# Row sums of W_tok: on VectorE from the rows as loaded, or on TensorE from the transposed matrix

## The chip, the core and the metric

The kernel runs on one core of a Trainium2 chip. A core has a matrix engine (TensorE, in the profile PE, with its weight loads as PEld), three engines for elementwise work (VectorE: DVE; ScalarE: ACT; GpSimd: POOL), a sync engine that issues transfers (SP), and 16 DMA engines. Each engine works through its own instructions in a fixed order and waits on semaphores for the others. Matmuls write to PSUM, eight banks of 2 KB per partition; everything else lives in SBUF, 128 partitions wide.

The metric is the device time of one launch in microseconds.

## The reference

Attention without softmax with a norm, then a block that mixes tokens and then channels (batch 8, 8 heads, 576 tokens, 64 per head, 512 channels, 2048 hidden):

```python
kv = np.einsum('bhsd,bhse->bhde', k, v)
out = np.einsum('bhsd,bhde->bhse', q, kv)
rms = np.sqrt(np.mean(out * out, axis=-1, keepdims=True) + 1e-06)
x = (out / rms * g_norm)            # then heads side by side: (8, 576, 512)
...
a1 = alpha1 * x + beta1
tok = np.einsum('ts,bsd->btd', w_tok, a1)
u = x + lam * tok
a2 = alpha2 * u + beta2
ch = np.maximum(a2 @ w_ch1, 0.0) @ w_ch2
return (u + lam * ch).astype(np.float32)
```

The part that matters here is `beta1`. In `tok` it gives for token t and channel d the value beta1[d] times the sum of row t of `w_tok`. So the kernel needs the 576 row sums of `w_tok`.

## The kernel before

**Tiling.** Tokens are the partitions: a batch is four chunks of 128 tokens and a tail of 64, and the tails of two batches share a tile. The token mixing contracts over tokens, so its stationary operand is W_tok transposed, `wt`: five slabs (chunks of s, the contracted token) by 576 columns (t), in bf16. Slab 4 has only 64 tokens in partitions 0 to 63 (and slab 5 holds the same with the halves swapped, for odd batches). Its other 64 partitions serve the beta1 term: the row operand `rtl` has lam*beta1 in partitions 64 and 96, and `wt` has the row sums there, rounded to bf16 in partition 64 and the rounding's remainder in partition 96. So beta1 rides along in the fifth matmul of each token mixing.

**Stages.** Batch 0 goes first and in halves of four heads (`qt_early`, `kv_first`, `norm_half`, `tok_half`, `a2_pair`), since its loads arrive piece by piece. W_tok is loaded as it lies (`wl`, in the space of the hidden activations `hh`), and `wt_group` transposes it with matmuls against an identity, five groups by source column block, each copied from PSUM to `wt` by ScalarE or VectorE (L982, L985); the last 64 rows gather in one bank (`wt_tail`, L978 and L990). Then `wsums` makes the row sums. After batch 0's token mixing the long part begins: two channel matmuls per batch (`ch1` L894, `ch2` L923), with the attention and token mixing of later batches woven between them.

**Row sums before.** `pick` is a 128x128 matrix with ones in columns 0, 32, 64 and 96. Five matmuls of `pick` with the slabs of `wt` (L1001) sum over s and leave the sums in partitions 0, 32, 64 and 96; five for t below 512 and five narrow ones for the rest. ScalarE copies partitions 64 to 127 to bf16 (L1008), VectorE writes the remainder into 96 to 127 (L1011). A memset (L500) clears that half of slab 4 first.

**The order.** The functions only record operations with their reads and writes. `ORDER` is a table of operation numbers, written out by hand or by a planner: `replay` takes the operations in that order, each engine getting its own in turn. `a:b` gives PSUM bank b, `a+b` weaves two groups of matmuls, and `~n` puts n dummy matmuls on a constant tile (`fil`, L446), which compute nothing that is used. `GATES` adds waits: the operation named first also waits for the second. Semaphore waits follow from reads, writes and bank reuse.

## Time and profile before

| | |
|---|---|
| median of 3 runs | 344.54 us (344.37 to 345.74) |
| the profiled execution | 343.25 us, its span 341.3 us |
| PE busy | 332.7 us, 97% |
| VectorE, ScalarE, POOL busy | 185.9, 148.8, 162.3 us |
| granted clock of TensorE | 1.00 throughout |
| first matmul of the channel part (L894) | 29.01 us |

In the rows of a timeline stand: start, duration of the row, engine, line, operation, output <- inputs, shapes, and xN for N merged instructions; in brackets the engine's idle time before it and what ended it. A matmul's row lasts until its data are out, so rows of PE overlap, and the pace of matmuls is read from start to start. In a row of stretches stand, after the stretch and its length, each engine's busy time with the number of its instructions. Rows of transfers give count, size and the time from issue to landing. The names of tiles are the program's allocations, so W_tok as loaded is called hh, its shared space.

### The profile page before, as it was taken

Reading aid. Unit: us, or ns where it says so; the run is one execution under the profiler, and the core shown is the slowest. Engines: PE = TensorE matmul, PEld = TensorE weight load, DVE = VectorE, ACT = ScalarE, POOL = GpSimd, SP = SyncE. Lnnn points to the kernel's source line nnn. Section 1 sums busy time; section 2 is a strip of 40 time slices with the busy share of each in tenths; the row PEclk is TensorE's granted clock in tenths of the full one; section 3 lists DMA queues with packets and bytes.
Section 4 is the critical chain, followed back from the end, with each engine's and each line's share of the span. In section 5 each row is a group of like instructions: output and inputs, shape, how many; then the busy total and the mean of one; then the engine's idle time right before and its main releaser. Section 6 shows DMA issues by size and latency. Waiting matters only on the chain.

```text
span 341.3 us, 5403 instructions
## 1 busy us (share of the span) xinstructions
PE 332.7 (97%) x2141; PEld 191.0 (56%) x2177; DVE 185.9 (54%) x346; ACT 148.8 (44%) x302; POOL 162.3 (48%) x154
## 2 busy tenths in 40 slices
PE   7999999999999999999999999999999999999996
PEld 7776653556555544555655555554576444444644
DVE  3694098424985796365744794458624963210044
ACT  5763663148603680336503572336325472026400
POOL 3699057572039608761087706932292607930000
PEclk9999999999999999999999999999999999999999
DMA  7999999999913991379723995399407530330013
GB/s 261 304 271 230 211 197 298 121 139 276 119 35 62 243 215 23 93 168 236 136 33 76 257 197 72 95 138 246 79 0 125 187 105 17 77 129 12 0 63 92
DMA packets 108496, 48.10 MB, mean 141 GB/s; under 512 B 82029, under 2 KB 101557, under 8 KB 108472
## 3 DMA queue, kind: packets, MB, share of 16 engines
q1 hardware_dynamic: 81648, 26.38, 40.6%
q0 software_dynamic: 26800, 21.38, 39.5%
q8 instruction: 17, 0.28, 0.4%
q14 instruction: 7, 0.06, 0.1%
q10 hardware_dynamic: 24, 0.01, 0.0%
HBM read 38.82 MB, written 9.44 MB: 141 GB/s over the span
## 4 chain that ended last, share of the span: by engine, by line
PE 79%; DVE 8%; DMA 4%; ACT 3%; SPq 2%; POOL 2%; issue 1%
PE ps L923 32%; PE ps L894 26%; PE ps L784 8%; PE ps L906 3%; DMA qs<-in_q_dram 3%; PE ps L701 2%; PE ps L611 2%; POOL a2b L881 2%; DMA w<-in_k_dram 1%; DVE ps L680 1%; DVE small L672 1%; PE ps L829 1%; SPq L1075 1%; PE ps L934 1%; PE ps L567 1%
## 5 line engine op out<-in xcount | busy, mean ns | idle before, releaser
L923 PE MATMUL ps<-w,hh 128*128 128x512 bf16 x543 | 134.1, 382 | 0.8 <-issue 0.2
L894 PE MATMUL ps<-a2m,w 128*128 128x512 bf16 x498 | 120.4, 381 | 0.6
L889 ACT ACTIVATE hh<-ps 128x512 bf16<-128x512 f32 x144 | 80.9, 598 | 71.0 <-PE ps L894 58.3
L923 PEld LDWEIGHTS ps<-w,hh 128*128 128x128 bf16 x560 | 48.2, 98 | 50.1 <-issue 0.8
L894 PEld LDWEIGHTS ps<-a2m,w 128*128 128x128 bf16 x512 | 46.5, 98 | 51.3 <-ACT hh L889 1.3
L874 POOL TENSOR_TENSOR a1f<-xm,a_bc 128x512 f32<-128x512 f32 x24 | 30.3, 1270 | 81.4 <-DVE xm L794 81.1
L951 DVE TENSOR_TENSOR tmp<-ps,lam_bc 128x512 f32<-128x512 f32 (+2 forms) x38 | 24.6, 658 | 52.6 <-PE ps L923 46.4
L956 POOL TENSOR_TENSOR xm<-xm,tmp 128x512 f32<-128x512 f32 x28 | 35.3, 1270 | 28.0 <-DVE tmp L951 28.0
L701 PE MATMUL ps<-kvc,qt 128*128 128x128 f32 x140 | 47.7, 406 | 0.7 <-ACT qt L1096 0.7
L881 POOL TENSOR_TENSOR a2b<-a1f,b_bc 128x512 bf16<-128x512 f32 x32 | 40.2, 1270 | 2.7 <-DVE a1f L878 1.8
L611 PE MATMUL ps<-vr,kr 128*128 128x128 f32 x112 | 38.2, 408 | 0.0
L672 DVE TENSOR_REDUCE small<-sq 128x8 f32<-128x512 f32 (+1 forms) x35 | 23.5, 677 | 24.5 <-ACT sq L669 24.0
L701 PEld LDWEIGHTS ps<-kvc,qt 128*128 128x128 f32 x140 | 27.4, 196 | 8.8 <-ACT qt L1096 0.9
L1096 ACT ACTIVATE qt<-qp 128x576 fp32r<-128x576 f32 x24 | 15.9, 679 | 36.9 <-DVE qp L1093 36.9
L669 ACT ACTIVATE sq<-ps 128x512 f32<-128x512 f32 (+1 forms) x35 | 20.5, 594 | 22.7 <-PE ps L701 22.6
L784 PE MATMUL ps<-rm,wt 128*128 128x512 bf16 x109 | 29.3, 381 | 0.9 <-DVE rtl L685 0.7
L794 DVE TENSOR_TENSOR xm<-ps,xm 128x512 f32<-128x512 f32 x24 | 16.3, 688 | 24.4 <-PE ps L784 23.4
L1093 DVE STREAM_TRANSPOSE qp<-qs 128x576 f32<-128x576 f32 x24 | 18.1, 765 | 13.2 <-ACT qt L1096 8.5
L611 PEld LDWEIGHTS ps<-vr,kr 128*128 128x128 f32 x112 | 22.0, 196 | 5.5
L680 DVE TENSOR_TENSOR ps<-ps,small 128x512 f32<-128x512 f32 (+1 forms) x35 | 23.8, 692 | 0.5
L687 DVE TENSOR_TENSOR xm<-ps,g_bc 128x512 f32<-128x512 f32 x28 | 18.6, 677 | 0.2
L906 PEld LDWEIGHTS ps<-a2l,w 128*128 128x128 bf16 x256 | 15.9, 98 | 3.8 <-ACT hh L889 0.2
(125 smaller groups left out, 295.7 us busy)
## 6 DMA issues: line engine op xcount, KB each, us to landing
out_dram<-xm SPq DMA_DIRECT2D x31, 256.0 KB, 2.7
kr<-in_k_dram POOLq DMA_DIRECT2D x7, 1024.0 KB, 8.2
vr<-in_v_dram POOLq DMA_DIRECT2D x7, 1024.0 KB, 10.0
qs<-in_q_dram SPq DMA_DIRECT2D x24, 288.0 KB, 7.2
w<-in_moe_w_ch_dram POOLq DMA_DIRECT2D x8, 512.0 KB, 9.4
xm<-in_q_dram SPq DMA_DIRECT2D x8, 288.0 KB, 5.2
qs<-in_v_dram SPq DMA_DIRECT2D x4, 288.0 KB, 5.5
w<-in_k_dram SPq DMA_DIRECT2D x4, 288.0 KB, 5.6
```

The lines of the kernel that those rows point to most:

```text
L611: P.mm("fill", 128, [lambda e, t=t, c=c, h=h, o=128 * (h % 4): e.matmul(t.ap()[:, o:o + 128], kr4[:, h, c:c + 2, :].rearrange("p c d -> p ...
L672: P.op("DVE", dve(n), lambda e: e.tensor_reduce(out=st, in_=sq[rs, s3, 0:nst, :], axis=AX.X, op=ALU.add), r=[("sq", s3)], w=[("sm", s4)])
L680: P.op("DVE", dve(n), lambda e: e.tensor_tensor(out=grp(ps()), in0=grp(ps()), in1=st[..., None].to_broadcast([rs.stop - rs.start, nst, DH] ...
L701: P.mm("fill", 128, [lambda e, p=p: e.matmul(dst(p), qt[:, p, cs], kvc[:, i, p, :], start=(p == 0), stop=(p == 3)) for p in range(4)], r=[ ...
L784: P.mm("fill", 512, [lambda e, sc=sc: e.matmul(t.ap(), wt[:, sc if sc < 4 else tw(b), 128 * c:128 * c + 128], rsrc(b, sc, al), start=(sc = ...
L874: P.op("POOL", pool(512), lambda e: e.tensor_tensor(out=a1f[:, s], in0=x, in1=a2_bc[:], op=ALU.mult), r=ks + ["a2"], w=[("a1f", s)])
L881: P.op("POOL", pool(512), lambda e: e.tensor_tensor(out=a2b[:, c], in0=a1f[:, s], in1=b2_bc[:], op=ALU.add), r=[("a1f", s), "b2"], w=[("a2 ...
L889: P.op("ACT", act(512), lambda e: e.activation(dst, t.ap(), ACT.Relu), r=[t], w=keys, pri=-1000)
L894: P.mm("main", 512, [lambda e, dj=dj: e.matmul(t.ap(), w1[:, dj, 128 * fj:128 * fj + 128], a2m[:, b % 3, dj, :], start=(dj == 0), stop=(dj ...
L906: P.mm("main", 128, [lambda e, dj=dj, fj=fj: e.matmul(t.ap()[:, 128 * fj:128 * fj + 128], w1[:, dj, 128 * (f4 + fj):128 * (f4 + fj) + 128] ...
L923: P.mm("main", 512, [lambda e, fj=fj, t=t, c=c: e.matmul(t.ap(), (ht[:, fj, 128 * c:128 * c + 128] if c < 4 else hl[:, fj, :]), w2[:, fj, ...
L956: lambda e: e.tensor_tensor(out=x, in0=x, in1=tmp[:, s, a:z], op=ALU.add),
```

## The change

VectorE sums the rows of W_tok as loaded (`wt_sums`, a reduction along the free dimension, for slabs 2 and 3, then 0 and 1, then the 64 rows of slab 4). It writes each sum, rounded to bf16, into padding column 576 of `wl`, and the remainder into column 608. The transposition of the last column block (columns 512 to 639) then carries them to partitions 64 and 96 of slab 4. `pick`, the ten matmuls, the copies and subtractions of sums and the memset of slab 4 are gone; slab 4 is copied in full, and `wt_tail` is one copy instead of two. The transpositions of the last block wait for the sums.

```diff
-        pick = sb("pick", [128, 128], BF16)
+        rsum = sb("rsum", [128, 5], F32)
...
-        P.op("DVE", dve(288), lambda e: e.memset(wt[64:128, 4, :].bitcast(F32), 0.0),
-             w=[("ws", 4), ("wst", 4)])
...
+            sums = [("wls", c) for c in (0, 2, 4)] if sc == 4 else []
             for tc in range(4):
                 P.mm("fill", 128, [lambda e, tc=tc: e.matmul(
                     t.ap()[:, 128 * tc:128 * tc + 128], wl[:, tc, cols], idb[:],
-                    start=True, stop=True)], r=["idb", "wlz", ("wl", tc)], w=[t])
+                    start=True, stop=True)], r=["idb", "wlz", ("wl", tc)] + sums[tc // 2:tc // 2 + 1], w=[t])
...
+        def wt_sums(c):
+            m, rs = 2 if c < 4 else 1, slice(0, 128 if c < 4 else 64)
+            src = [("wl", c), ("wl", c + 1)] if c < 4 else ["wlt"]
+            P.op("DVE", dve(576 * m), lambda e: e.tensor_reduce(
+                rsum[rs, c:c + m], wl[rs, c:c + m, 0:576], op=ALU.add, axis=AX.X), r=src,
+                w=[("rs", c)])
+            P.op("DVE", dve(m), lambda e: e.tensor_copy(
+                out=wl[rs, c:c + m, 576], in_=rsum[rs, c:c + m]), r=["wlz", ("rs", c)],
+                w=[("wls", c)])
+            P.op("DVE", dve(m), lambda e: e.tensor_tensor(
+                out=wl[rs, c:c + m, 608], in0=rsum[rs, c:c + m], in1=wl[rs, c:c + m, 576],
+                op=ALU.subtract), r=["wlz", ("rs", c), ("wls", c)], w=[("wls", c)])
...
-                P.mm("fill", n, [lambda e, sc=sc, t=t, a=a, z=z, n=n: e.matmul(
-                    t.ap()[:, 0:n], pick[:, :], wt[:, sc, a:z], start=(sc == 0), stop=(sc == 4))
-                    for sc in range(5)],
...
             if j == 0:
+                for c in (2, 0, 4):
+                    wt_sums(c)
                 for sc in range(5):
                     P.bias = 5.0 + 2 * sc
                     wt_group(sc)
```

`ORDER` and `GATES` are new as well, as in their first lines:

```diff
-13 0 3 6 30 4 31 ~32 14 7 1 32 12 9 28 5 8 208 10 36 11 27 21 37 35 20 34 29 19 49 43:1 48 ~5 18
+12 0 3 7 206 4 ~39 13 6 27 14 9 1 8 33 207 10 11 30 32 17 46 31 18 28 26 29 16 45 5 25 21 34
...
-GATES = {23: 53, 39: 68, 40: 74, 41: 164, 125: 152, 126: 214, 205: 197, 234: 270, 235: 217, 236:
+GATES = {23: 50, 38: 141, 39: 12, 124: 243, 203: 328, 204: 184, 205: 342, 233: 322, 234: 213, 235:
```

The order differs up to about the middle of the program and is the same from there on. Lines of the changed kernel lie 5 lower in the places below (L758 is L753 there, L982 is L978). Three places follow, each as it stood and as it stands.

VectorE, from the norm of batch 0's first half (xm) to the copies of the transposed W_tok (CAST wt), with the semaphores waited for; d_16 and d_17 are the landings of W_tok's two large transfers. Before:

```order
L758 TENSOR_TENSOR xm<-ps,small 128x2x256 [waits s_DVE] x2
L601 TENSOR_TENSOR kvc<-ps,g_bc 64x64 [waits s_ACT] x2
L757 RECIPROCAL small<-small 64x4
L758 TENSOR_TENSOR xt<-ps,small 64x256 [waits s_DVE]
L601 TENSOR_TENSOR kvc<-ps,g_bc 64x64 [waits s_ACT] x2
L500 MEMSET wt 64x288
L1127 MEMSET kr 64x512
L982 CAST wt<-ps 128x512 [waits s_PE]
```

Now, between the same two:

```order
L988 TENSOR_REDUCE rsum<-hh 128x2 [waits d_17]
L596 TENSOR_TENSOR kvc<-ps,g_bc 64x64 [waits s_ACT]
L988 TENSOR_REDUCE rsum<-hh 128x2 [waits d_16]
L596 TENSOR_TENSOR kvc<-ps,g_bc 64x64
L991 CAST hh<-rsum 128x2 [waits s_DVE]
L991 CAST hh<-rsum 128x2
L994 TENSOR_TENSOR hh<-rsum,hh 128x2 [waits s_DVE] x2
L596 TENSOR_TENSOR kvc<-ps,g_bc 64x64 [waits s_ACT]
L752 RECIPROCAL small<-small 64x4
L596 TENSOR_TENSOR kvc<-ps,g_bc 64x64
L753 TENSOR_TENSOR xt<-ps,small 64x256 [waits s_DVE]
L978 CAST wt<-ps 128x512 [waits s_PE]
```

Two reductions and four small operations came in, two memsets went out.

PE at the same place, from batch 0's second k-v product (qs, w) to its token mixing (rm, wt); fil are the dummies, idb with hh the transpositions of W_tok. Before:

```order
L446 MATMUL ps<-fil 128x128 x2
L567 MATMUL ps<-ident,tmp 128x128 x9
L975 MATMUL ps<-idb,hh 128x128 x2
L446 MATMUL ps<-fil 128x128 x3
L975 MATMUL ps<-idb,hh 128x128 x18
L727 MATMUL ps<-kvc,qt 128x4x64 x10
L1001 MATMUL ps<-wt,pick 128x512 x5
L807 MATMUL ps<-rm,wt 128x256 x16
```

Now:

```order
L562 MATMUL ps<-ident,tmp 128x128
L445 MATMUL ps<-fil 128x128 x11
L971 MATMUL ps<-idb,hh 128x128
L562 MATMUL ps<-ident,tmp 128x128 x8
L445 MATMUL ps<-fil 128x128 x17
L971 MATMUL ps<-idb,hh 128x128 x4
L445 MATMUL ps<-fil 128x128 x11
L971 MATMUL ps<-idb,hh 128x128 x10
L722 MATMUL ps<-kvc,qt 128x4x64 x2
L971 MATMUL ps<-idb,hh 128x128
L722 MATMUL ps<-kvc,qt 128x4x64 x4
L971 MATMUL ps<-idb,hh 128x128 x4
```

The matmuls with pick are gone, and dummies stand among the transpositions, 92 in the whole program instead of 47.

GpSimd, from the first scaled rows of batch 0 (rm) to the last (rtl), with the loads that it issues between them: w is the first channel weight, kr and vr are the next batch's k and v, xm and qp copies of the next batch's q. Before:

```order
L763 TENSOR_TENSOR rm<-xm,la_bc 128x2x256 [waits s_DVE]
L763 TENSOR_TENSOR rtl<-xt,la_bc 64x256 [waits s_DVE]
L1083 DMA kr<-in_k_dram 128x8x256
L1060 DMA w<-in_moe_w_ch_dram 128x4x512
L763 TENSOR_TENSOR rm<-xm,la_bc 128x2x256
L563 COPY xm<-xm 128x9x64 [waits d_29]
L563 COPY qp<-xm 128x9x64 [waits d_30]
L563 COPY qp<-xm 128x9x64 [waits d_28]
L563 COPY xm<-xm 128x9x64 [waits d_31]
L1083 DMA vr<-in_v_dram 128x8x256
L763 TENSOR_TENSOR rm<-xm,la_bc 128x2x256 [waits s_DVE] x2
L763 TENSOR_TENSOR rtl<-xt,la_bc 64x256
```

Now:

```order
L758 TENSOR_TENSOR rm<-xm,la_bc 128x2x256 [waits s_DVE] x2
L1052 DMA w<-in_moe_w_ch_dram 128x4x512 x2
L1075 DMA vr<-in_v_dram 128x8x256
L558 COPY xm<-xm 128x9x64 [waits d_29]
L758 TENSOR_TENSOR rtl<-xt,la_bc 64x256 [waits s_DVE]
L558 COPY qp<-xm 128x9x64 [waits d_28]
L558 COPY qp<-xm 128x9x64 [waits d_30]
L558 COPY xm<-xm 128x9x64 [waits d_31]
L1075 DMA kr<-in_k_dram 128x8x256
L1052 DMA w<-in_moe_w_ch_dram 128x4x512
L758 TENSOR_TENSOR rm<-xm,la_bc 128x2x256 [waits s_DVE] x2
L758 TENSOR_TENSOR rtl<-xt,la_bc 64x256
```

Three loads of w instead of one stand between them. On ScalarE, the second copy of batch 0's q (L560 in the kernel before) stands ahead of the squares of its first half (L749), not behind them; and the first large transfer of W_tok is gated by the last of ScalarE's three first copies to qt instead of the second.

More of the change, by code (lines that the diff above doesn't have):

```diff
@@ L495, in bass_transnormer_attn__then__resmlp_affine_kernel @@
         P.op("DVE", dve(128), lambda e: e.memset(one[:], 1.0), w=["one"])
-        P.op("DVE", dve(64), lambda e: e.memset(pick[:], 0.0), w=["pick"])
         P.op("DVE", dve(160), lambda e: e.memset(wl[:, :, 576:640].bitcast(F32), 0.0), w=["wlz"])
@@ L976, in wt_group @@
                     t.ap()[:, 128 * tc:128 * tc + 128], wl[:, tc, cols], idb[:],
-                    start=True, stop=True)], r=["idb", "wlz", ("wl", tc)], w=[t])
+                    start=True, stop=True)], r=["idb", "wlz", ("wl", tc)] + sums[tc // 2:tc // 2 + 1], w=[t])
             P.mm("fill", 64, [lambda e: e.matmul(
                 wtt.ap()[:, 64 * sc:64 * sc + 64], wl[:, 4, cols], idb[:, 0:64],
-                start=True, stop=True)], r=["idb", "wlt", "wlz"], w=[wtt])
+                start=True, stop=True)], r=["idb", "wlt", "wlz"] + sums[2:], w=[wtt])
@@ L981, in wt_group @@
             if sc % 2:
                 P.op("DVE", dve(512), lambda e: e.tensor_copy(
[L983 removed]
+                    out=wt[:, sc, 0:512], in_=t.ap()), r=[t], w=[("wt", sc)])
             else:
                 P.op("ACT", act(512), lambda e: e.activation(
[L986 to L993 removed]
@@ L995, in wsums @@
[L995 to L1014 removed]
+                    wt[:, sc, 0:512], t.ap(), ACT.Identity), r=[t],
@@ L1015, in wsums @@
+        def wt_tail():
+            P.op("ACT", act(320), lambda e: e.activation(
+                wt[:, 0:5, 512:576],
+                wtt.ap()[:, 0:320].rearrange("p (c t) -> p c t", t=64),
+                ACT.Identity), r=[wtt], w=[("wtt", i) for i in range(5)] + [("wst", 4)])
+        def wsums():
             for a, z, key in ((0, 64, ("ws", 5)), (64, 0, ("wt", 5))):
```

35 lines of the change are left out of this document (8 added, 27 removed), and 139 rows, old and new, of tables (GATES, ORDER).

## The prediction

> **What bounds the kernel now.** I read the page first, then busy time by stretches, then the timeline of each engine over the first 30 us, since every edit that is not a moved row lies there.
>
> ```profile
> span 341.3 us, 5403 instructions
> PE 332.7 (97%) x2141; PEld 191.0 (56%) x2177; DVE 185.9 (54%) x346; ACT 148.8 (44%) x302; POOL 162.3 (48%) x154
> ```
>
> TensorE (PE) is busy 97% of the span; no other engine reaches 56%. By that average a change which takes ten matmuls off PE and gives work to a half-idle VectorE (DVE) looks like a gain. The stretches say otherwise:
>
> ```profile
> core 0: us, PE busy (x) PEld busy (x) DVE busy (x) ACT busy (x) POOL busy (x), PEclk, DMA share, GB/s
> 15.60:18.00 2.40, 2.27 (x32) 1.99 (x31) 1.98 (x10) 2.35 (x7) 2.30 (x3) 1.00 1.05 361
> 18.00:25.40 7.40, 6.95 (x54) 5.40 (x55) 7.13 (x15) 4.41 (x11) 7.37 (x10) 1.00 1.19 254
> 25.40:29.00 3.60, 3.55 (x39) 3.23 (x39) 2.37 (x4) 1.80 (x6) 3.60 (x6) 1.00 1.29 278
> 29.00:341.30 312.30, 306.44 (x1809) 168.81 (x1842) 167.35 (x295) 130.88 (x259) 141.94 (x125) 1.00 0.78 128
> ```
>
> From 18.0 to 25.4 us VectorE is busy 7.13 of 7.40 us, and GpSimd (POOL) 7.37 and then 3.60 of 3.60 us: they are the tight engines there, while PE still has small holes. From 29 us on PE alone is the limit, and it has the same matmuls before and after. So the change is worth what it moves the start of the long PE stretch, the first L894 matmul, plus what the new order does to PE's few later waits.
>
> The timeline of PE on the way there:
>
> ```profile
> 16.75 1.17 PE L975 MATMUL ps<-idb,hh 128*128 128x128 bf16 x18
> 17.73 1.72 PE L727 MATMUL ps<-kvc,qt 128*128 128x256 f32 x10
> 19.61 1.02 PE L1001 MATMUL ps<-wt,pick 128*128 128x512 bf16 x4 [0.16 <-issue]
> 20.47 2.18 PE L807 MATMUL ps<-rm,wt 128*128 128x256 bf16 x16
> ...
> 25.46 0.63 PE L849 MATMUL ps<-ident,xm 128*128 128x128 f32 x4
> ...
> 28.64 0.31 PE L1001 MATMUL ps<-wt,pick 128*128 128x64 bf16 x5
> 29.01 0.81 PE L894 MATMUL ps<-a2m,w 128*128 128x512 bf16 x3
> ```
>
> And of VectorE:
>
> ```profile
> 10.08 0.34 DVE L601 TENSOR_TENSOR kvc<-ps,g_bc 64x64 fp32r<-64x64 f32 x2 [5.29 <-ACT kvc L599]
> ...
> 12.63 1.28 DVE L752 TENSOR_REDUCE small<-sq 128x8 f32<-128x512 f32 x2 [1.29 <-ACT sq L749]
> ...
> 13.94 0.36 DVE L752 TENSOR_REDUCE small<-sq 64x4 f32<-64x256 f32 x1
> ...
> 14.40 1.24 DVE L758 TENSOR_TENSOR xm<-ps,small 128x512 f32<-128x512 f32 x2
> ...
> 15.81 0.15 DVE L757 RECIPROCAL small<-small 64x4 f32<-64x4 f32 x1
> ...
> 16.83 0.30 DVE L500 MEMSET wt<- 64x288 f32 x1
> 17.18 0.48 DVE L1127 MEMSET kr<- 64x512 f32 x1
> 17.96 1.29 DVE L982 CAST wt<-ps 128x512 bf16<-128x512 f32 x2 [0.29 <-PE ps L975]
> ...
> 21.68 0.70 DVE L1011 TENSOR_TENSOR wt<-ps,wt 32x512 bf16<-32x512 f32 x1
> ...
> 24.07 1.27 DVE L818 TENSOR_TENSOR xm<-ps,xm 128x512 f32<-128x512 f32 x2
> ```
>
> The reader is to see three things. From the first L982 (17.96) to the end of the pair of L818 (24.07 + 1.27 = 25.34) VectorE runs without a gap worth naming: 7.38 us. The first L849 on PE starts at 25.46, 0.12 us after that pair, since it transposes what they wrote. And from that L849 to the first L894 PE is full: 29.01 - 25.46 = 3.55 us. So the path to the start of the long stretch is VectorE up to 25.34, then PE.
>
> **The change part by part.**
>
> *Ten matmuls away.* The five wide ones hold PE from 19.61 to 20.47, 0.86 us; this lies while VectorE is the limit, so it shortens nothing there. The five narrow ones hold it from 28.64 to 29.01 minus the gap, about 0.31 us; this lies on the PE path: -0.31 us. Off ScalarE go two copies of sums, off VectorE two subtractions.
>
> *Row sums on VectorE.* Before the first L982 of the new order stand two reductions of 128x1152 (two slabs of 576). No row shows one; the nearest are L752. Two of 512 elements take 1.28, so 0.64 each, one of 256 takes 0.36: 1.09 ns an element, hence 0.64 + 640 x 0.00109 = 1.34 us each, 2.68 for both. From below, an engine that took two of these 16-bit elements at once would need about half, 0.67 each; from above, 2.25 times 0.64 is 1.44. I take 1.34, by the slope of the same operation on the same engine. The Trainium skill, page "VectorE: DVE Perf Modes", section "The perf-mode tier table", says that tensor_reduce has only its 1x form, whatever the type; by that rule the 16-bit source buys nothing, the sum below stands and the halved price falls away. No row of before can confirm it, since all its reductions read 32-bit data.
>
> *Four small operations* (two casts, two subtractions of 128x2) follow the reductions, each one waiting for VectorE's own last result. The nearest row is the reciprocal of 64x4, 0.15 us: 0.60 us in all, between 0.2 (if they overlap) and 0.8.
>
> *Two memsets leave this place*: L500 is gone, the one of kr is among the first instructions now, where VectorE later idles 5 us anyway. From 16.83 to 17.66 they took 0.83 us. The wait of 0.29 for PE before L982 is used up as well. The third reduction (64x576, 0.36 + 320 x 0.00109 = 0.71) stands between the two L982 and takes the place of the wide L1011 (0.70): nothing. Its cast and subtraction come after the first two L818, behind which L849 no longer waits: nothing, as long as the second pair of L818 is still waiting for PE.
>
> So the first L982, and with it the VectorE path, moves by 2.68 + 0.60 - 0.83 - 0.29 = +2.16 us.
>
> *A copy moved on ScalarE.*
>
> ```profile
> 12.00 1.34 ACT L749 ACTIVATE sq<-ps 128x512 f32<-128x512 f32 x3 [0.27 <-PE ps L727]
> ...
> 14.15 0.67 ACT L560 ACTIVATE tmp<-xm 128x576 f32<-128x576 f32 x1
> ```
>
> The L560 copy now stands ahead of the L749 squares, whose results the reductions at 12.63 wait for. Of its 0.67 us, 0.27 is hidden in the wait shown; the rest would delay VectorE by 0.4. The wait for the narrow matmul of PE may end slightly earlier, so I take +0.25 (bounds 0 and 0.4).
>
> *W_tok's arrival.* The sums read W_tok as loaded, so they wait for its two large transfers, which the matmuls did only through the transpositions.
>
> ```profile
> 8.23 1.61 POOL L481 DMA_DIRECT2D hh<-in_moe_w_tok_dram  x2 [2.71 <-ACT g_bc L530]
> ...
> hh<-in_moe_w_tok_dram POOLq DMA_DIRECT2D x1, 288.0 KB, 6.4
> ...
> hh<-in_moe_w_tok_dram POOLq DMA_DIRECT2D x1, 288.0 KB, 7.2
> ```
>
> They land at 8.23 + 6.4 = 14.6 and about 9.1 + 7.2 = 16.3. The first reduction cannot start before L758 ends, 15.64 + 0.25 = 15.9, the second about 17.4. Their issue moves back by some 1 us, since the gate now is the last of ScalarE's three first copies to qt; even if the landings moved as far (15.6 and 17.3), both are in time. Cost nothing, cover 0.1 to 0.3 us; 0.3 at the upper end.
>
> *POOL's queue.* Two more loads of w1 now stand ahead of the second pair of rm products.
>
> ```profile
> 15.13 1.27 POOL L763 TENSOR_TENSOR rm<-xm,la_bc 128x512 bf16<-128x512 f32 x1 [1.59 <-DVE xm L758]
> ...
> 18.11 0.76 POOL L1060 DMA_DIRECT2D w<-in_moe_w_ch_dram  x1
> ...
> 25.98 0.75 POOL L763 TENSOR_TENSOR rtl<-xt,la_bc 64x256 bf16<-64x256 f32 x1
> 26.65 1.56 POOL L1060 DMA_DIRECT2D w<-in_moe_w_ch_dram  x2
> ```
>
> POOL is full from 15.13 to 26.7. Two issues by half of 1.56 are +1.56, and its start moves by 0.25 with L758: the last rm product, which ended about 25.98, ends near 27.8. The L807 matmuls that read it stand 1.0 us behind the first L849, in the shifted run at 25.46 + 2.16 + 0.25 + 1.0 = 28.9. So POOL is hidden, by 1.1 us of cover. Should VectorE turn out quicker, POOL is next: L807 at 27.8, and with 2.2 us of PE work between it and L894, that start is at 30.0, still +1.0.
>
> *Fillers.* PE has 92 instead of 47 of its dummy matmuls L446. They stand where PE waits, so they cost nothing of their own while the VectorE path is the later one: 2.4 us of cover, which 45 x 0.056 = 2.5 nearly uses up (by the 18 matmuls of L975, the same 128x128 shape, from 16.75 to 17.73: 0.054 us each, rounded up). Bound 0 to +0.3.
>
> *The rest of the order.* After L894 the units stand in a new order up to about the middle of the program, and in the old one from there; the matmuls are the same, and the distances in matmuls between one stage's results and the next one's use are nearly so. PE waits there by name in two places:
>
> ```profile
> 54.32 0.61 PE L784 MATMUL ps<-rm,wt 128*128 128x512 bf16 x2 [0.40 <-DVE rtl L685]
> ...
> 82.49 0.33 PE L701 MATMUL ps<-kvc,qt 128*128 128x128 f32 x1 [0.69 <-ACT qt L1096]
> ```
>
> Both wait for work that PE's own earlier matmuls feed, so a later start moves both sides alike. I take 0, bounds -1.1 (both gone) and +0.8 (a new one of that size).
>
> **Sum:** +2.16 + 0.25 - 0.31 = +2.1 us. The profiled execution took 343.25 us (span 341.3 and 1.95 around it), so its like would take 345.35. The median of the runs shown is 344.54, 1.29 above the profiled one; put on that, 346.6 us.
>
> **Rivals.** A (not slower): PE's busy time is what counts. VectorE's new work would fit its idle time (5.29 us before the first L601), and the end moves by the matmuls removed: -0.86 - 0.31 = -1.2 us, 343.4; with the two later waits gone too, 342.3. For it speaks the 97%; against it that the sums stand behind L758 in VectorE's order, past that idle time, and the 0.12 us between L818 and L849. It decides if the first L982 starts by about 18.0 us.
> B: reductions of 16-bit data at twice the rate. VectorE's path then gains 1.34, but POOL holds the start: +1.0, 345.5.
> C: the later half of the opening gives time back: both later waits vanish in the new order, 2.1 - 1.1 = +1.0, 345.5. For it: the order was made anew; against: their feeders shift with PE.
> D: a new wait of the later order, or W_tok landing later than its cover, on top of the forecast: +2.9, 347.4.
>
> **How the numbers follow.** Forecast 0.50, with its own range of +1.3 to +2.8 (the small operations, ScalarE's copy and the fillers at their ends), 345.8 to 347.3; A 0.13, B 0.10, C 0.13, D 0.14. A measurement of this kernel tells about 0.5%, 1.7 us, from no change. Slower by more: D whole, the forecast's part above 1.7 (three quarters, 0.38), a little of B and C (0.05): 0.57. Faster by more: A with the waits gone, 0.09. Within: the rest, 0.34. Range: from A's 343.4 with a little of its better end, 343.0, to D with half as much again, 348.4.
>
> **What would show it.** In the profile of the changed kernel: the reductions at about 1.34 us each; the first cast of wt on VectorE near 20.4 instead of 17.96; the first L849's successor near 27.9, the first channel matmul near 31.1; PE's later waits no larger than the two shown. The forecast is wrong if the reductions take half, if the first cast starts near 18, or if the first channel matmul is 2 us later and the span is not, which would mean that the later stages gave it back.

## The result and the profile after

The changed kernel takes 346.22 us in the median of 20 runs (344.13 to 347.14), the kernel before 344.48 us beside it (20 runs, 343.1 to 345.74). The medians differ by 1.74 us, where 2.1 were forecast. The ratio of the runs, estimated with its interval, is 1.0043 (95% interval 1.0027 to 1.0058); here and below it is not simply that of the medians, which is 1.0050 here. The profiled execution of before (343.25 us) lies near the fast end of its runs and that of after (346.05 us) near the median of its own, so the two profiles differ by 2.80 us where the medians differ by 1.74.

The changed kernel's busy time in the long stretch (columns as in the prediction):

```profile
32.05:344.10 312.05, 306.48 (x1809) 168.97 (x1842) 167.15 (x294) 132.14 (x259) 140.31 (x124) 1.00 0.79 127
```

The long stretch begins at 32.05 us, where the first channel matmul starts, and lasts 312.05 us with the same 1809 matmuls; before it began at 29.01 and lasted 312.30. So all that was lost was lost in the opening, +3.04 us in these two executions; the new order behind it gave back 0.25 us at most.

VectorE in the changed kernel's opening, out of its timeline:

```profile
15.41 1.34 DVE L988 TENSOR_REDUCE rsum<-hh 128x2 f32<-128x1152 bf16 x1
...
16.80 1.34 DVE L988 TENSOR_REDUCE rsum<-hh 128x2 f32<-128x1152 bf16 x1
...
18.19 0.23 DVE L991 CAST hh<-rsum 128x2 bf16<-128x2 f32 x2
18.38 0.24 DVE L994 TENSOR_TENSOR hh<-rsum,hh 128x2 bf16<-128x2 f32 x2
...
20.29 0.69 DVE L978 CAST wt<-ps 128x512 bf16<-128x512 f32 x1
...
26.10 1.29 DVE L813 TENSOR_TENSOR xm<-ps,xm 128x512 f32<-128x512 f32 x2 [0.27 <-PE ps L802]
...
27.48 2.38 DVE L994 TENSOR_TENSOR hh<-rsum,hh 64x1 bf16<-64x1 f32 x1
...
30.98 0.79 DVE L849 TENSOR_SCALAR a2m<-ps,ab 128x512 bf16<-128x512 f32 x1
```

The two reductions take 1.34 us each, to the hundredth what was forecast. The Trainium skill's rule that the reduction has only its 1x form (page "VectorE: DVE Perf Modes", section "The perf-mode tier table") agrees: the 16-bit source bought nothing. The first cast of wt starts at 20.29 (forecast 20.4). But one row was not in the forecast at all: the subtraction of the last 64 sums, one element in each of 64 partitions, stands for 2.38 us. The earlier subtractions, twice as many elements in twice as many partitions, took 0.24 us for both. Behind it in VectorE's order wait two casts of q and then L849, which writes the a2m that the first channel matmul reads.

PE, POOL and SP at the same place:

```profile
16.87 0.22 PE L971 MATMUL ps<-idb,hh 128*128 128x128 bf16 x1 [0.97 <-DMA hh<-in_moe_w_tok_dram]
...
17.80 1.11 PE L445 MATMUL ps<-fil 128*128 128x128 bf16 x17
...
18.98 0.78 PE L445 MATMUL ps<-fil 128*128 128x128 bf16 x11
19.59 0.72 PE L971 MATMUL ps<-idb,hh 128*128 128x128 bf16 x10
...
24.40 0.33 PE L562 MATMUL ps<-ident,qp 128*128 128x128 f32 x1 [0.76 <-POOL qp L558]
...
27.90 1.07 PE L844 MATMUL ps<-ident,xm 128*128 128x128 f32 x8
29.21 1.05 PE L802 MATMUL ps<-rm,wt 128*128 128x256 bf16 x8 [0.23 <-POOL rm L758]
...
32.05 0.81 PE L889 MATMUL ps<-a2m,w 128*128 128x512 bf16 x3 [0.46 <-DVE a2m L849]
```

```profile
23.67 0.67 POOL L558 COPY qp<-xm 128x576 f32<-128x576 f32 x1 [1.81 <-DMA xm<-in_q_dram]
...
26.60 2.55 POOL L758 TENSOR_TENSOR rm<-xm,la_bc 128x512 bf16<-128x512 f32 x2
29.08 0.75 POOL L758 TENSOR_TENSOR rtl<-xt,la_bc 64x256 bf16<-64x256 f32 x1
```

```profile
14.43 3.87 SPq L461 DMA_DIRECT2D xm<-in_q_dram x4
```

Four larger waits of PE are new: for W_tok itself (0.97), for a copy of q by POOL (0.76), for the second rm products (0.23) and for the a2m product (0.46). POOL's copy waited 1.81 us for a load of q, whose issue on SP's queue had been slow: four issues in 3.87 us, of which the third took 2.31 (15.51 to 17.82), so that the fourth load landed at 23.62. And the long subtraction runs from 27.48 to 29.86, while POOL multiplies from 26.60 to 29.83: it ends with POOL's third product.

### The profile page after: what moved, and what is told of

Read it like the earlier page. It is cut to its first block, busy times and chain, and to the rows that moved or that the text cites. A ratio compares the mean times of both kernels' runs of the same rounds, so it can differ in the third digit from the quotient of the medians.

```text
span 344.1 us, 5472 instructions
## 1 busy us (share of the span) xinstructions
PE 334.7 (97%) x2177; PEld 193.7 (56%) x2212; DVE 190.2 (55%) x350; ACT 149.5 (43%) x299; POOL 162.1 (47%) x154
## 4 chain that ended last, share of the span: by engine, by line
PE 85%; DVE 7%; ACT 3%; DMA 2%; POOL 1%; SPq 1%; issue 1%
PE ps L918 33%; PE ps L889 28%; PE ps L779 9%; PE ps L901 4%; PE ps L696 3%; PE ps L606 2%; DMA xm<-in_q_dram 2%; DVE ps L675 1%; PE ps L824 1%; PE ps L445 1%; PE ps L929 1%; SPq L461 1%; DVE small L667 1%; ACT hh L884 1%; DVE xm L682 1%
## 5 line engine op out<-in xcount | busy, mean ns | idle before, releaser
L889 PE MATMUL ps<-a2m,w 128*128 128x512 bf16 x498 | 120.7, 381 | 1.1 <-DVE a2m L849 0.5
L889 PEld LDWEIGHTS ps<-a2m,w 128*128 128x128 bf16 x512 | 46.6, 98 | 51.4 <-ACT hh L884 1.2
L664 ACT ACTIVATE sq<-ps 128x512 f32<-128x512 f32 (+1 forms) x35 | 20.4, 591 | 23.4 <-PE ps L696 23.3
```

Of the source, the lines that this page charges most:

```text
L889: P.mm("main", 512, [lambda e, dj=dj: e.matmul(t.ap(), w1[:, dj, 128 * fj:128 * fj + 128], a2m[:, b % 3, dj, :], start=(dj == 0), stop=(dj ...
```

## The experiments

After the result the theory had two parts. T1: VectorE's sums move the start of the long stretch, as forecast. T2: the long subtraction reads two tensors from SBUF and is held while POOL multiplies. Rivals: the sums are hidden and POOL's queue sets the start; W_tok's landing sets it; PE's busy time counts. All ratios below are to the kernel before on the same chip, with the 95% interval; behind "Measured" stands the median of 12 runs, or of the single execution where a probe was run once.

**1. The tail's remainder from one tensor.** The same value, with the sum given as a per-partition scalar:

```diff
+            if c == 4:
+                P.op("DVE", dve(m), lambda e: e.tensor_scalar(
+                    out=wl[rs, c:c + m, 608], in0=wl[rs, c:c + m, 576], scalar1=rsum[rs, c:c + 1],
+                    scalar2=-1.0, op0=ALU.subtract, op1=ALU.mult), ...
```

> The changed kernel, but the remainder of the last 64 row sums is written by a VectorE operation with one tensor input (the sum enters as a per-partition scalar) in the same place. In the changed kernel this 64x1 subtraction of two SBUF tensors took 2.38 us, from 27.48 to 29.86, and ended with GpSimd's last product at 29.83. Theory (two tensor inputs from SBUF make VectorE wait while GpSimd computes): it takes about 0.15 us, the wait of 0.46 us ahead of the first channel matmul goes, that matmul starts near 31.4 instead of 32.05, the time falls by about 0.6 us against the changed kernel (ratio to the kernel before near 1.003). Rival (the operation waits for something else, such as its own predecessor's write): it stays at 2.4 us and the time stays.

Measured: 345.05 us, ratio 1.0012 (0.9987 to 1.0036); the medians are level (345.14 us for the kernel before on that chip).

```profile
27.04 0.21 DVE L995 TENSOR_SCALAR hh<-hh,rsum 64x1 bf16<-64x1 bf16 x1
```

```profile
30.15 1.03 PE L889 MATMUL ps<-a2m,w 128*128 128x512 bf16 x4
```

The first fence is VectorE, the second PE. 0.21 us instead of 2.38, and the channel part starts at 30.15 without a wait. (In this execution no load of q was late either, so the 1.9 us between the two profiles aren't the subtraction's alone.)

**2. Short sums.** The reductions read 64 of 576 columns.

```diff
-                rsum[rs, c:c + m], wl[rs, c:c + m, 0:576], op=ALU.add, ...
+                rsum[rs, c:c + m], wl[rs, c:c + m, 0:64], op=ALU.add, ...
```

> The changed kernel with each row sum taken over 64 of 576 columns, so the row sums are incomplete; all else stands. The two reductions shrink from 1.34 to about 0.15 us each. Theory of the prediction (VectorE's reductions set the first copy of the transposed W_tok): that copy starts about 2 us earlier, at 18.0 to 18.5 instead of 20.3, and the first channel matmul 1.0 us or more earlier. Rival (PE waits in its order for W_tok's landing at 16.7, ScalarE and VectorE behind it, so that the sums are half hidden): the copy stays within 0.3 us of 20.3, and the time within 0.4 us of the changed kernel.

Measured: 346.17 us, ratio 1.0038 (1.001 to 1.0066): nothing gained, though each reduction fell to 0.27 us. VectorE and PE:

```profile
17.95 1.26 DVE L991 CAST hh<-rsum 128x2 bf16<-128x2 f32 x2
...
20.84 0.69 DVE L978 CAST wt<-ps 128x512 bf16<-128x512 f32 x1
...
27.49 2.45 DVE L994 TENSOR_TENSOR hh<-rsum,hh 64x1 bf16<-64x1 f32 x1
```

```profile
17.41 0.23 PE L971 MATMUL ps<-idb,hh 128*128 128x128 bf16 x1
```

The first cast of wt came later than both theory and rival had it. Part of that is the execution: its opening ran late from the start (last section), and the first reduction stands at 17.04 us instead of 15.41. Two other things hold the start here. The tail's subtraction is long again, and now the casts of 128x2 are too (1.26 us; they took 0.23), beside the first rm products of POOL, which ended at 19.11. And the first cast of wt stands 3.43 us behind PE's first transposition of W_tok, as it does in the changed kernel (20.29 - 16.87 = 3.42). Experiment 7 takes that up.

**3. The first transposition of W_tok moved behind those of q,** so that PE doesn't wait for W_tok (in the order, operation 93 behind 130).

> The changed kernel with one matmul moved in PE's order: the first transposition of W_tok stands behind the eight transpositions of q, not ahead of them, so that these don't wait for W_tok's landing. Theory of the prediction: the reductions set the pace, nothing gained, first copy of the transposed W_tok at 20.3. Rival (W_tok's landing in PE's order): the eight transpositions start near 15.9 instead of 16.9, ScalarE's copies follow 0.9 us earlier, the small VectorE product at 19.09 moves to about 18.65, the first copy to about 19.85, and the first channel matmul by 0.3 to 0.45.

Measured: 346.19 us, ratio 1.0037 (1.0015 to 1.006): nothing gained. The profile can't tell what PE's wait was worth, since a load of v landed late in that execution (at 14.19 us, in the changed kernel at 12.08) and the transpositions of q began at 17.36 for that reason. The first cast of wt came at 21.31 and the first channel matmul at 31.23, behind small operations that were long once more; VectorE, and POOL beside it:

```profile
19.02 0.51 DVE L991 CAST hh<-rsum 128x2 bf16<-128x2 f32 x2
19.21 1.01 DVE L994 TENSOR_TENSOR hh<-rsum,hh 128x2 bf16<-128x2 f32 x2
```

```profile
17.96 1.57 POOL L1052 DMA_DIRECT2D w<-in_moe_w_ch_dram  x2
19.52 0.91 POOL L1075 DMA_DIRECT2D vr<-in_v_dram  x1
```

The two casts and two subtractions took 1.20 us together; in the changed kernel they took 0.43. POOL multiplied nothing then: its first rm products had ended at 18.0, and it was issuing loads. So T2 as it stands is too narrow: an operation of VectorE can be held with POOL multiplying nothing. The second cast and the first subtraction ended at 19.53, together with one of POOL's issues, which points to these, but no probe tests it. And in the changed kernel and in experiment 1 the same four stood beside the same issues and took their usual time.

**4. The kernel before with one `pick` matmul in place of five,** in each of the two groups.

> The kernel before with one matmul instead of five in each of the two groups that make row sums (L1001), so the row sums are incomplete; copies and subtractions stay. Theory: the wide group lies under VectorE's work, only the narrow one counts, a gain of at most 0.3 us, ratio to the kernel before between 0.999 and 1.0. Rival (PE's busy time is what counts): four fifths of 0.86 + 0.31 us, a gain of 0.9 us, ratio 0.9975.

Measured: 343.47 us, ratio 0.9963 (0.9937 to 0.999), where 0.999 to 1.0 was expected by the theory and 0.9975 by the rival. Its profile (343.15 us) shows the channel part starting at 28.97, as before. So the profiles give the theory's answer and the timed runs more than the rival's; this stays open.

**5. Two loads of w1 back behind the second rm products** on POOL's queue, with the one-input remainder (operations 192 and 193 behind 166).

> The changed kernel with the tail remainder taken from one tensor input, and the second and third load of w1 put back on POOL's queue behind the second set of rm products, where they stood before the change. Theory (VectorE sets the start of the long stretch, POOL is the next limit): with one tensor input the second pair of L818 products ended at 26.95 us and POOL's second rm products at 27.78; without the two issues (0.75 us each) POOL's end moves to about 26.3 and VectorE and PE hold the start alone: first channel matmul at 29.9 to 30.2 us, ratio to the kernel before 0.999 to 1.002, nothing gained on the run with one tensor input. Rival (POOL's queue holds the start and the sums do not): first channel matmul near 29.0, ratio 0.997 to 0.999.

Measured: 345.12 us, ratio 1.0011 (0.9989 to 1.0032), first channel matmul at 30.25 us. As the theory had it (30.25 is 0.05 above its range): with the subtraction short, POOL's two issues cost nothing that can be seen.

**6. All small operations in one-tensor form,** one column each, on top of experiment 5, and POOL's product of one row (L511, called a copy below) ahead of the third load of W_tok, so that SP's queue gets on sooner.

```diff
+            def each(f):
+                return lambda e: [f(e, k) for k in range(c, c + m)][-1]
...
+            P.op("DVE", dve(m), each(lambda e, k: e.tensor_copy(
+                out=wl[rs, k:k + 1, 576], in_=rsum[rs, k:k + 1])), ...
+            P.op("DVE", dve(m), each(lambda e, k: e.tensor_scalar(
+                out=wl[rs, k:k + 1, 608], in0=wl[rs, k:k + 1, 576], scalar1=rsum[rs, k:k + 1],
+                scalar2=-1.0, op0=ALU.subtract, op1=ALU.mult)), ...
```

> The kernel of the run before this one, with all small operations written for one column and one tensor input each (128x1 casts, remainders by a per-partition scalar), twice as many, and with POOL's copy of the row for one constant (line 511 of the changed kernel) put ahead of the third load of W_tok, so that SP's queue issues the loads of q earlier. Theory (an operation that reads two tensors from SBUF, or a 128x2 cast, stands still while POOL multiplies; none of these forms does): no small operation over 0.3 us in the first 32 us, POOL's wait for a load of q (1.81 us in the changed kernel's profile) gone; four more small operations cost up to 0.5 us, so the first channel matmul lies at 29.9 to 30.6 us, ratio 0.998 to 1.002. Rival (the long subtraction has another cause, a wait for its own operand): some of the small ones still take over 1 us.

Measured: 344.40 us, ratio 0.9991 (0.9971 to 1.0011): level with the kernel before.

```profile
18.79 0.32 DVE L994 CAST hh<-rsum 128x1 bf16<-128x1 f32 x4
19.03 0.57 DVE L997 TENSOR_SCALAR hh<-hh,rsum 128x1 bf16<-128x1 bf16 x4
```

No small operation is long, and POOL no longer waits for q. The first channel matmul came at 30.82 us, 0.2 later than expected; a load of v had landed late in this execution too, at 13.97.

**7. The same with short sums.**

> The same with reductions over the first 64 of 576 columns, so the sums, and all that is worked out from them, are incomplete; number and order of the operations stand. The two reductions ahead of the first cast of wt fall from 1.34 to 0.27 us each. Theory (with the small operations and POOL's queue out of the way, the sums themselves are what is left): the first cast of wt comes 2.1 us earlier than in the run before this one, the first channel matmul 1.4 to 2.1 us earlier, and the ratio to the kernel before is 0.4 to 0.6 hundredths lower than there. Rival (POOL's products, or W_tok's landing, hold the start as well): the cast moves, the first channel matmul by less than 0.7 us, and the ratio by less than 0.2 hundredths.

Measured: 344.03 us, ratio 0.9988 (0.9967 to 1.0009), against 0.9991 with whole sums: the rival's answer. VectorE had its sums and small operations done at 18.75 (at 19.60 with whole sums, though this execution had reached them 1.05 us later), and yet:

```profile
20.84 0.69 DVE L978 CAST wt<-ps 128x512 bf16<-128x512 f32 x1
```

The first transposition on PE had started at 17.40: 3.44 us again. Between the first and the last of W_tok's transpositions ahead of the cast stand 28 dummy matmuls (the rows of 17 and 11 in the result's profile; from start to start they hold PE 0.95 + 0.61 us). In the kernel before, this distance was 17.96 - 16.48 = 1.48 us. So a second chain, from W_tok's landing through PE's dummies to the cast, has almost the length of VectorE's. In the changed kernel it was even the one that released the first cast: 3.42 or 3.43 us is the distance in its two profiles and in those of experiments 2, 5 and 6.

**8 and 9. Without the 28 dummies,** with whole sums and with short ones (in the order, `~17` and the `~11` behind it are dropped).

> The run with one-column operations and the whole sums, less the 17 and 11 dummy matmuls that stand on PE between the first and the last transposition of W_tok's rows. Ground: in every profile so far the first cast of wt came 3.4 us after the first of these transpositions on PE (changed kernel 16.87 and 20.29, one-input run 16.72 and 20.23, short sums 17.41 and 20.84, short sums with one-column operations 17.40 and 20.84), however VectorE stood; in the kernel before it was 16.48 and 17.96. Theory now (two chains of almost one length: VectorE with the sums, and PE from W_tok's landing through the 28 dummies, 1.7 us): without the dummies VectorE's chain alone holds; its cast comes 0 to 0.5 us earlier than with them, the ratio is lower by 0 to 0.15 hundredths than 0.9991. Rival (PE's row alone is what the change costs, the sums are hidden): the cast comes 1.4 to 1.7 us earlier, counted from the first transposition, the ratio is 0.994 to 0.996.

> The same without the 28 dummies, and with the sums over 64 of 576 columns only (incomplete sums, so all that is worked out from them is too). Theory (two chains): only with both out of the way does the opening get shorter: cast of wt 1.3 to 1.7 us after where the run with the 28 dummies and short sums had it becomes 1.3 to 1.7 us before, counted from the first transposition (2.0 instead of 3.43 us); first channel matmul at 28.8 to 29.8 us; ratio 0.994 to 0.997 to the kernel before. Rival (POOL's second rm products hold the start whatever VectorE does): the cast moves, the first channel matmul stays within 0.4 us, ratio 0.998 to 0.9995.

Measured: 345.23 us, 1.001 (0.9983 to 1.0037), and 344.94 us, 1.0003 (0.9981 to 1.0025). Whole sums, PE and then VectorE:

```profile
16.70 0.22 PE L971 MATMUL ps<-idb,hh 128*128 128x128 bf16 x1 [0.40 <-DMA hh<-in_moe_w_tok_dram]
...
18.55 0.40 PE L971 MATMUL ps<-idb,hh 128*128 128x128 bf16 x4 [0.76 <-ACT qt L575]
```

```profile
20.50 0.67 DVE L978 CAST wt<-ps 128x512 bf16<-128x512 f32 x1
```

Short sums:

```profile
18.39 1.10 PE L971 MATMUL ps<-idb,hh 128*128 128x128 bf16 x14 [0.76 <-ACT qt L575]
...
29.70 0.81 PE L889 MATMUL ps<-a2m,w 128*128 128x512 bf16 x3
```

```profile
18.76 0.23 DVE L596 TENSOR_TENSOR kvc<-ps,g_bc 64x64 fp32r<-64x64 f32 x1 [1.17 <-ACT kvc L594]
...
19.82 0.67 DVE L978 CAST wt<-ps 128x512 bf16<-128x512 f32 x1
```

With whole sums, taking the dummies out moves the cast from 20.89 to 20.50 and does not lower the ratio (1.001 against 0.9991): VectorE holds alone. That part of the two-chain theory stood. With both out of the way the channel part started 0.94 us sooner than with whole sums (29.70 against 30.64), within what was expected (28.8 to 29.8). But the ratio didn't follow (1.0003; 0.994 to 0.997 was expected), and the cast comes 3.28 us behind the first transposition (16.54), not 2.0: PE now waits 0.76 us for ScalarE's copy of q and VectorE 1.17 us for ScalarE's copy of k-v products. A third chain, through ScalarE, is only 0.7 us shorter (cast at 19.82). The medians differ by 0.3 us, within the error. In the two profiles the earlier start was given back: behind the first channel matmul the short sums' kernel took 1.19 us longer, most of it in two waits of PE that the other doesn't have (0.33 and 0.54 us); whether its other executions have them too isn't known. The four runs with and without sums and dummies together say that the sums themselves are worth at most about a microsecond here.

**10. The hold by itself,** in one execution. The kernel before, with probes on VectorE whose results nobody reads, some beside POOL's nine products in a row, some where POOL is idle:

```diff
+            P.op("DVE", 0.2, lambda e: e.tensor_tensor(
+                out=prb[0:64, 8:9], in0=prb[0:64, 0:1], in1=prb[0:64, 1:2], op=ALU.subtract), ...
+            P.op("DVE", 0.2, lambda e: e.tensor_scalar(
+                out=prb[0:64, 9:10], in0=prb[0:64, 0:1], scalar1=prb[0:64, 1:2], ...
+            P.op("DVE", 0.2, lambda e: e.tensor_copy(out=prw[:, 0:2, 32], in_=prb[:, 2:4]), ...
+            P.op("DVE", 0.2, lambda e: e.tensor_copy(out=prw[0:64, 4:5, 32], in_=prb[0:64, 4:5]), ...
```

> The kernel before, with eight extra operations on VectorE whose results nobody reads, on a tile of their own: a difference of two 64x1 tensors, the same by a per-partition scalar (one tensor input), a cast of 128x2 and a cast of 64x1. One set stands where POOL runs nine products in a row (98.98 to 110.11 us in the profile of before: the one-input forms and the casts at about 100.7, the two-input difference at about 105.5), one where POOL is idle (about 119 us). Theory (two tensor inputs from SBUF, and the 128x2 cast, wait for POOL): in the idle set all four take under 0.2 us; beside the products the one-input form and the 64x1 cast take the same, the 128x2 cast and the two-input difference 1 us or more, up to the end of the nine products. Rival (their place in the changed kernel or their operands made them long): all eight under 0.3 us.

VectorE beside the products, and then with POOL idle:

```profile
100.25 0.17 DVE L1180 TENSOR_SCALAR prb<-prb 64x1 f32<-64x1 f32 x1
100.34 0.14 DVE L1185 CAST prw<-prb 64x1 bf16<-64x1 f32 x1
100.40 0.79 DVE L1183 CAST prw<-prb 128x2 bf16<-128x2 f32 x1
...
105.13 0.98 DVE L1177 TENSOR_TENSOR prb<-prb 64x1 f32<-64x1 f32 x1
```

```profile
118.69 0.15 DVE L1183 CAST prw<-prb 128x2 bf16<-128x2 f32 x1
118.76 0.14 DVE L1177 TENSOR_TENSOR prb<-prb 64x1 f32<-64x1 f32 x1
```

POOL's products at that time (the two before the first row began at 98.65):

```profile
101.12 2.51 POOL L883 TENSOR_TENSOR a2b<-a1f,b_bc 128x512 bf16<-128x512 f32 x2
...
106.05 2.50 POOL L883 TENSOR_TENSOR a2b<-a1f,b_bc 128x512 bf16<-128x512 f32 x2
```

The two-tensor difference and the 128x2 cast are held (0.98 and 0.79 us instead of 0.14 and 0.15), the one-tensor form and the 64x1 cast are not. Both ended where one of POOL's products gave way to the next, at 101.19 and 106.11. So the hold beside products, T2 but for its limits, is shown apart from this change. The Trainium skill has the rule (page "SBUF — State Buffer", section "Who interferes with whom"): VectorE's second read port is shared with GpSimd, an operation with two SBUF inputs or in a two-port mode contends for it, and whoever has it keeps it for its whole instruction. By that rule a hold would last 1.27 us at most (an estimate: the length of one product here); the 2.38 and 2.45 us above went past that.

**11. How long the hold lasts:** six two-tensor differences at other places of the kernel before, in one execution.

> The kernel before with six differences of two 64x1 tensors on VectorE, nobody reading their results: one behind the first pair of L818 products, beside three rm products of POOL that wait for nothing between them; four beside the nine products of 98.98 to 110.11 us, of which three start in the first product of a pair; one where POOL is idle. Question: why the changed kernel's subtraction stood 2.38 us, past the ends of two products, when the first probe stood 0.98 us to the end of one. Theory a (the wait lasts to the end of the product that runs): no probe above 1.3 us, the first one ends near 26.1. Theory b (it lasts while POOL goes from product to product without a wait of its own): the first one lasts to the end of the third product, near 26.8, and those that start in the first product of a pair take up to 2.5 us. The one beside no product: under 0.2 us by both.

VectorE, and POOL beside it:

```profile
26.65 1.71 DVE L1179 TENSOR_TENSOR prb<-prb 64x1 f32<-64x1 f32 x1
```

```profile
25.12 2.54 POOL L765 TENSOR_TENSOR rm<-xm,la_bc 128x512 bf16<-128x512 f32 x2
27.59 0.76 POOL L765 TENSOR_TENSOR rtl<-xt,la_bc 64x256 bf16<-64x256 f32 x1
```

The first probe passed the change of products at 27.6 and ended with the third, at 28.36, as in the changed kernel. The four beside the nine products took 0.38 to 0.72 us, each to the end of the product that ran. So a hold can pass over a change of products, but need not.

**12. The changed kernel again.**

> The changed kernel once more, unaltered, for a second profile and a second ratio to set beside the runs with the tail remainder from one tensor input (1.0012 and 1.0011) and with all small operations so (0.9991). Theory (the subtraction with two tensor inputs, held while POOL goes through its second rm products, makes up half or more of the loss): the subtraction of the tail takes over 1 us again, the ratio is 1.003 to 1.0055. Rival (the first ratio was high by chance, the change costs what the one-input run shows): ratio 1.000 to 1.002.

Measured: 345.59 us, ratio 1.0031 (0.9995 to 1.0066): between theory and rival, its interval holds both. Its profiled execution took 344.37 us, 1.68 us less than the first, by the same program. VectorE, PE, POOL and SP:

```profile
27.32 0.45 DVE L994 TENSOR_TENSOR hh<-rsum,hh 64x1 bf16<-64x1 f32 x1
```

```profile
30.42 1.03 PE L889 MATMUL ps<-a2m,w 128*128 128x512 bf16 x4
```

```profile
25.23 2.52 POOL L758 TENSOR_TENSOR rm<-xm,la_bc 128x512 bf16<-128x512 f32 x2 [0.38 <-DVE xm L753]
```

```profile
14.02 2.11 SPq L461 DMA_DIRECT2D xm<-in_q_dram x4
```

Two executions of one program, side by side: the four issues of q took 2.11 us here and 3.87 there. Here q is in time, POOL's second rm products start at 25.23 instead of 26.60, the subtraction falls into the second of them and is held 0.45 us instead of 2.38, and the channel part starts at 30.42 instead of 32.05. That is 1.63 of the 1.68 us. The stages read so: the first pair of L844 is 0.62 later (27.90 against 27.28, PE's wait for q); L802 another 0.38 (29.21 against 28.21, less the 0.62); L889 the last 0.63, the hold. So in these profiles a hold of 2.38 us costs 0.63, and one of 0.45 nothing that can be seen.

**The runs together.** Four measurements have the two-tensor subtraction of the tail (the changed kernel twice, experiments 2 and 3): 1.0043, 1.0038, 1.0037, 1.0031. Six have it in one-tensor form (experiments 1 and 5 to 9, two of them with short sums): 1.0012, 1.0011, 1.0010, 1.0003, 0.9991, 0.9988. The groups don't overlap, whatever else differs within them; their means are 1.0037 and 1.0003. The difference, 0.0035 or 1.2 us (1.1 by the medians), is most of what the change cost. It is argued from groups and not shown for the subtraction alone: experiment 1 is the only one that differs from the changed kernel by that form alone, and its interval overlaps those of the changed kernel; four of the six have the other small operations changed too; and the tail was held long in two of the four profiles, 0.45 us in the other two. The best of the six with whole sums (0.9991) can't be told from the kernel before; none beats it.

## Why the prediction was right, and where it was not

The forecast was 346.6 us (+2.1); the measurement is 346.22 (+1.74), in the likeliest case's own range. Of the three chances it is a narrow call: 1.0043 lies just within the 0.5%, to which I gave 0.34, while its interval reaches beyond, to which I gave 0.57. And part of the sum came out by two errors of opposite sign, which is luck.

- *The opening decides, PE's busy time doesn't.* Right. Rival A asked for a first cast by about 18.0; it came at 20.29 and 20.49. The long stretch kept its length (312.05 against 312.30), as "the rest of the order" said, so C fell as well. (PE had four waits in that stretch, not two; the other two are of 0.29 and 0.16 us.) Against it stands experiment 4, whose gain A would explain better.
- *Reductions of 1.34 us each, four small operations 0.60.* Right: 1.34 and 1.34; 0.43 for the small ones (18.19 to 18.62). B fell. The first cast was forecast at 20.4 and came at 20.29 and 20.49. That it fits so well is in part luck: VectorE was ready some 0.06 us sooner, and PE's transpositions released the cast, 3.42 us behind the first of them, which had waited for W_tok's landing.
- *The third reduction's "cast and subtraction come after the first two L818 ... nothing".* This step failed. I named L849 (the transposition, L844 now) as the only one who waits and looked no further down VectorE's order, where the a2m product stands that the first channel matmul reads; and I priced the subtraction by its size. It stood for 2.38 us in one execution, where it cost 0.63, and for 0.45 in the other, where it cost nothing. By the groups of runs, this term and the holds of the other small operations are worth about 1.1 to 1.2 us together.
- *VectorE's +2.16 as the change of the end.* The size is right at the first cast and too large at the end. In the repeat, where nothing was held for long, the cast was 2.53 later than before, the end of the pair of L813 1.88 (27.22 against 25.34: the same number of operations, 15, followed each other more closely), the channel part 1.41 and the execution 1.12 us. In the medians of the six one-tensor kernels even that is missing (1.0003). So the sum was about right since the term left out stood in for a term that was too large.
- *The narrow matmuls, -0.31.* Right: from the first L849 to the first L894 3.55 us before, 30.42 - 27.28 = 3.14 in the repeat, -0.41.
- *The copy moved on ScalarE, +0.25.* The delay was there but didn't reach the sum: the squares started 0.97 us after their product on PE (10.90 to 11.87) instead of 0.75 (11.25 to 12.00), but that product came 0.35 sooner, and the first L747 started at 12.49 instead of 12.63.
- *W_tok's arrival, nothing.* Not quite. In the first execution the reductions didn't wait for it, in the repeat the first one did (0.32), and PE's first transposition waited in both (0.97 and 1.45), a wait that the prediction doesn't price. It costs nothing that can be seen only because VectorE arrives at the same time, as experiments 7 to 9 show.
- *POOL's 1.1 us of cover.* Used up in the first execution by something I hadn't looked at: POOL waits for q, q waits for SP's queue, and SP's queue waits for a POOL product of one row (L511) that the new order has put behind W_tok's three issues. In the repeat the cover held, with 0.46 us left (27.75 to 28.21).
- *Fillers, 0 to +0.3.* Right as a cost (1.001 without 28 of them), and by the margin stated: 2.5 us of them against 2.4 of cover leave none, and PE's chain with them is as long as VectorE's.
- *The upper end of the range* doesn't follow from its own words: D with half as much again is 344.54 + 4.35 = 348.9, not 348.4.

What stays open, besides how the hold ends, is why the medians of the one-tensor kernels show none of the 1.1 us or so by which their profiled executions (344.09 to 344.75) stand behind that of before (343.25). One profile of a kernel whose executions spread over 3 us says little by itself. One thing fits and isn't shown: in some executions PE starts slowly (last section). In the kernel before, the first cast of wt stood at 17.96 without a slow start and at 19.31 with one (experiment 11), while in the kernels of experiments 2 and 7, with such a start, it came at 20.84, no later than the 20.89 of experiment 6 without one. Where W_tok's landing sets the pace, a slow start would be hidden. Experiment 4's gain is the other thing left unexplained.

## What to carry to other kernels

When small work moves to an engine that looks half idle, price it by its neighbours and not by its size: a one-element operation with two SBUF operands can stand behind another engine's large ones. Follow the order behind it down to the first result that the bounding engine reads. And where several chains have nearly one length, shortening one shows nothing: only with two shortened at once did the channel part start sooner here (by 0.94 us), and even then the time didn't fall.

## What the runs showed of the hardware

- A VectorE difference of two 64x1 SBUF tensors takes 0.14 us with POOL idle and 0.38 to 2.45 beside POOL's products; a 128x2 cast 0.15, and 0.79 and 1.19 beside products; a 64x1 cast and a one-tensor form by a per-partition scalar stay at 0.14 and 0.17 to 0.21. While POOL issued loads, 128x2 casts took up to 0.45 us and two-tensor differences of 128x2 up to 0.66 (experiment 3), or no more than usual (the changed kernel, experiment 1). The hold ended with the product that ran six times in the probes and once each in experiment 3 and in the repeat, and passed over one or two changes of products in the changed kernel, in experiment 2 and in the first probe of experiment 11. What decides between the two is open.
- PE's first 10 us come at two speeds, in executions of the same code. The first 36 of the k-v products, in the kernel before and in experiment 11, whose code up to there differs by one memset on VectorE, and the granted clock in that stretch of the latter:

```profile
7.05 1.26 PE L589 MATMUL ps<-qs,w 64*64 64x64 f32 x36 [0.39 <-DMA w<-in_k_dram]
```

```profile
7.86 2.09 PE L591 MATMUL ps<-qs,w 64*64 64x64 f32 x36
```

```profile
4.50:10.00 5.50, 5.30 (x56) 4.60 (x54) 0.27 (x3) 3.46 (x6) 2.08 (x4) 1.00 1.03 379
```

The clock reads 1.00 in both. The Trainium skill, page "TensorE: Matmul & The Clock Gate", section "What's actually happening", says that the array runs at half its clock until a free-running window has seen it busy; that fits the two speeds and their coming and going, and the column of the granted clock does not show it here.
- Four issues of q on SP's queue took 2.11 and 3.87 us in two executions of one program. The slower one is where the 1.6 us between the two profiles of the changed kernel begin; what stretched it was not found.
